# A mixture-of-experts kernel: first-layer products whose width follows the expert's token count

## The chip, the cores and the metric

The program runs on one core of a Trainium2 chip. The metric is device time in microseconds (us) for one execution; the smaller the better. TensorE (PE in the profile, with its weight loads shown apart as PEld) multiplies, ScalarE (ACT), VectorE (DVE) and GpSimd (POOL) work on tiles, and SyncE (SP) issues transfers. A `q` behind an engine's name in a row marks what its sequencer does itself: semaphore waits, register loads, branches.

## The reference

Three stages follow each other: an attention block (4 batches, 8 heads, 576 positions), a gated MLP, and a mixture of experts. The change lies in the last one:

```
logits = einsum('bsd,de->bse', x, w_gate)             # 8 experts
e = argmax(logits[b, s]), or the expert of the position before (sticky gate)
h = maximum(x[b, s] @ w1[e], 0.0)                     # 512 -> 1024, first layer
out[b, s] = p[e] * (h @ w2[e])                        # 1024 -> 512, second layer
```

There are 4 x 576 = 2304 tokens, and each goes to one of the 8 experts. How many an expert gets is known only when the program runs. Worked out with the reference on the inputs of its default seed, experts 0 to 7 get 227, 356, 289, 239, 277, 278, 294 and 344 tokens.

## The kernel before

Attention and the MLP fill the first two thirds of the span. In that time the routing of each batch (`route`) gives every token a place in its expert's list and adds the batch's counts to the tile `carry` (L1133; a row for each partition, summed over partitions by a product with ones). An expert has room for `CAP` = 3 blocks of 128 tokens, `CC` = 384 columns, in the static part; a loop at the end (`overflow`, L1190 and L1191) would handle what does not fit.

Per expert, `gather` fetches the 3 blocks of token rows by an indirect transfer on GpSimd's queue, `xT` transposes them on TensorE (L1287) into a rounded half and a rest (`xt[:, 0]`, `xt[:, 1]`), `L1` makes the first layer and `L2` the second. `L1` works in 8 groups of 128 hidden units; each group is one accumulation of 12 products (4 slices of the 512 inputs, 3 products each) over 384 columns, followed by Relu on ScalarE (L1300) and the rest on VectorE (L1301). `L2` works in 3 blocks of 128 tokens, each 24 products of 512 columns (L887 is the line of `mm3`, the helper that issues nearly all products), then a scaling on ScalarE and an indirect store. There are 7 rotating accumulator tiles (`ps`) and one for small results (`rt`, through `rs()`).

Weights come in pieces of 512 KB (`load_w`): a transfer into one of 2 raw tiles, a cast on ScalarE (L1256), the rest on VectorE (L1257), into one of 10 `wp` tiles; an expert has 8 pieces, 0 to 3 for the first layer, 4 to 7 for the second. Expert 0 is handled apart and early (2 blocks in `early_L1`, the third by `L1_rows`); experts 1 to 7 run in the loop of `experts`. A scheduler orders each engine's instructions by data and by order of emission; in the program text all 4 first-layer pieces of expert e + 1 follow `L1` of expert e, and its 4 second-layer pieces follow `L2`.

Of the kernel before, what the change touches and what calls it, by code (L numbers as in the profile page):

```python
# [8 lines left out]
F32 = mybir.dt.float32  # L9
F32R = mybir.dt.float32r  # L10
BF16 = mybir.dt.bfloat16
I32 = mybir.dt.int32
ACTF = mybir.ActivationFunctionType
ALU = mybir.AluOpType
# [10 lines left out]
def f32v(ap):  # L25
    return ap.bitcast(F32)
# [7 lines left out]
def kernel(  # L34
# [19 lines left out]
    PE, ACT, DVE, POOL, SP = nc.tensor, nc.scalar, nc.vector, nc.gpsimd, nc.sync  # L54
# [5 lines left out]
    E = w_gate.shape[1]  # L60
# [4 lines left out]
    KD = DM // 128  # L65
# [16 lines left out]
    def behind(x, name):  # L82

        tc.add_manual_dep(
            x.ins, name, mybir.DependencyInfo(mybir.DependencyClass.NoSync, mybir.DependencyReason.DATA), reason="after"
        )
# [8 lines left out]
    def ps(tag="ps", bufs=7):  # L95
        t = psum.tile([128, 512], F32, tag=tag, name=tag, bufs=bufs)
        return t

    def rs():
        return ps("rt", 1)  # L100
# [15 lines left out]
    def T(pool, shape, dt, tag, bufs=1):  # L116
        _n[0] += 1
        return pool.tile(shape, dt, tag=tag, name=f"{tag}_{_n[0]}", bufs=bufs)
# [19 lines left out]
    onesb = T(const, [128, 128], BF16, "onesb")  # L138
# [5 lines left out]
    carry = T(const, [128, E], BF16, "carry")  # L144
# [740 lines left out]
    def mm3(pt, pairs, first_, last_):  # L885
        n = len(pairs)
        ms = [PE.matmul(pt, lhsT=l, rhs=r, start=(first_ and x == 0), stop=(last_ and x == n - 1)) for x, (l, r) in enumerate(pairs)]  # L887
        return ms
# [353 lines left out]
    WP = {}  # L1242

    def load_w(e, j):

        r = T(wpool, [128, 1024], F32, "wraw", bufs=2)
        if j < KD:
            dma(r, w1[e, 128 * j:128 * j + 128, :])
        else:
            f0 = 256 * (j - KD)  # L1250
            x = dma(r.rearrange("p (a d) -> p a d", a=2), w2[e, f0:f0 + 256, :].rearrange("(a p) d -> p a d", p=128))
            if e == 0:
                behind(x, m_loads[LPN])
        near = (e * 2 * KD + j) % (WA + WB) < WA
        w = T(wpool if near else epool[0], [128, 2, 1024], F32R, "wp", bufs=WA if near else WB)
        c = ACT.copy(out=w[:, 0, :], in_=r)  # L1256
        a = DVE.tensor_tensor(out=w[:, 1, :], in0=r, in1=f32v(w[:, 0, :]), op=ALU.subtract)  # L1257
        if (0, KD) <= (e, j) < (1, KD):
            behind(a, dmarks[-1].ins.name)
        if (1, 0) < (e, j) < (1, 2 * KD):  # L1260
            behind(c, amarks[1 if j < KD else 3].ins.name)
        WP[e, j] = w

    CC = CAP * 128
# [10 lines left out]
    def gather(e):  # L1275
        for blk in range(CAP):
            c = e * NBLK + blk
            x = fetch(xgs[e % 2][:, blk, :], ids[:, c:c + 1])
        return x.ins.name

    def xT(xt, xg, n0, n):

        w = 128 * n
        for kt in range(KD):
            pt = ps()
            for blk in range(n):
                PE.transpose(pt[:, 128 * blk:128 * blk + 128], xg[:, n0 + blk, 128 * kt:128 * kt + 128], ident)  # L1287
            ACT.copy(out=xt[:, 0, kt, 0:w], in_=pt[:, 0:w])
            DVE.tensor_tensor(out=xt[:, 1, kt, 0:w], in0=pt[:, 0:w], in1=f32v(xt[:, 0, kt, 0:w]), op=ALU.subtract)

    def L1(e, xt, ht, w_, after={}):
        for f in range(NF):
            pt = ps()
            fs = slice(128 * f, 128 * f + 128)
            for kt in range(KD):
                w = WP[e, kt]
                ms = mm3(pt[:, 0:w_], [(w[:, 0, fs], xt[:, 0, kt, 0:w_]), (w[:, 0, fs], xt[:, 1, kt, 0:w_]), (w[:, 1, fs], xt[:, 0, kt, 0:w_])], kt == 0, kt == KD - 1)
                if kt == 0 and f in after:
                    behind(ms[0], after[f].ins.name)
            ACT.activation(out=ht[:, 0, f, 0:w_], in_=pt[:, 0:w_], func=ACTF.Relu)  # L1300
            DVE.scalar_tensor_tensor(out=ht[:, 1, f, 0:w_], in0=pt[:, 0:w_], scalar=0.0, in1=f32v(ht[:, 0, f, 0:w_]), op0=ALU.max, op1=ALU.subtract)  # L1301
            yield 12 * w_ * 0.42

    def L2(pool, e, ht, t, prob, idx):
        of = out.rearrange("b s d -> (b s) d")
        pt = ps()
        ts_ = slice(128 * t, 128 * t + 128)
        for f in range(NF):
            w = WP[e, KD + f // 2].rearrange("p z (a d) -> p z a d", a=2)[:, :, f % 2, :]
            mm3(pt, [(ht[:, 0, f, ts_], w[:, 0, :]), (ht[:, 0, f, ts_], w[:, 1, :]), (ht[:, 1, f, ts_], w[:, 0, :])], f == 0, f == NF - 1)  # L1310
        y = T(pool, [128, DM], F32, "y", bufs=3)
        ACT.activation(out=y, in_=pt, func=ACTF.Copy, scale=prob)  # L1312
        POOL.indirect_dma_start(  # L1313
            out=of[:, :], out_offset=bass.IndirectOffsetOnAxis(ap=idx, axis=0), in_=y, in_offset=None,
            bounds_check=NT - 1, oob_is_err=False,
        )
# [27 lines left out]
    def L1_rows(pool, e, xt, ht):  # L1344

        hs = []
        for z in range(2):
            fs = slice(512 * z, 512 * z + 512)
            pt = ps()
            for kt in range(KD):  # L1350
                w = WP[e, kt]
                mm3(pt, [(xt[:, 0, kt, 0:128], w[:, 0, fs]), (xt[:, 0, kt, 0:128], w[:, 1, fs]), (xt[:, 1, kt, 0:128], w[:, 0, fs])], kt == 0, kt == KD - 1)
            hs.append(T(pool, [128, 512], F32, "y", bufs=3))
            amarks.append(ACT.activation(out=hs[z], in_=pt, func=ACTF.Relu))
            yield 1
        for z in range(2):
            pt = ps()
            for f in range(4):
                PE.transpose(pt[:, 128 * f:128 * f + 128], hs[z][:, 128 * f:128 * f + 128], ident)
            pv = pt.rearrange("p (f t) -> p f t", f=4)  # L1360
            d = slice(4 * z, 4 * z + 4)
            amarks.append(ACT.copy(out=ht[:, 0, d, 0:128], in_=pv))
            DVE.tensor_tensor(out=ht[:, 1, d, 0:128], in0=pv, in1=f32v(ht[:, 0, d, 0:128]), op=ALU.subtract)  # L1363
            yield 1

    def next_w(e, js):
        for j in js:
            if e < E and (e, j) not in WP:
                load_w(e, j)

    def experts(pool):
        xts = {}

        def new_xT(e, n0=0):
            xts[e] = T(pool, [128, 2, KD, CC], F32R, "xT", bufs=2)
            xT(xts[e], xgs[e % 2], n0, CAP - n0)

        def new_hT():
            return T(pool, [128, 2, NF, CC], F32R, "hT", bufs=1)

        def early_L2(t):
            L2(pool, 0, early["ht"], t, early["xg"][:, t, DM:DM + 1], ids0[:, t:t + 1])

        next_w(0, range(2 * KD))
        early_L2(0)
        xts[0] = T(pool, [128, 2, KD, CC], F32R, "xT", bufs=2)
        xT(xts[0], early["xg2"].unsqueeze(1), 0, 1)
        ht0 = new_hT()
        rows = L1_rows(pool, 0, xts[0], ht0)
        next(rows), next(rows)  # L1390
        early_L2(1)
        next(rows), next(rows)
        for e in range(E):
            if 0 < e < E - 1:
                g = gather(e + 1)
            if e == 3:
                emit_olist(pool, g)
            xt = xts.pop(e)
            t0 = 0 if e else CAP - 1
            ht = new_hT() if e else ht0  # L1400
            if e:
                for _ in L1(e, xt, ht, CC):
                    pass
            for j in range(KD):
                WP.pop((e, j))
            if e + 1 < E:
                next_w(e + 1, range(KD))
                new_xT(e + 1)
            for t in range(t0, CAP):
                c = e * NBLK + t  # L1410
                xg = xgs[e % 2][:, t] if e else early["xg2"]
                L2(pool, e, ht, t - t0, xg[:, DM:DM + 1], ids[:, c:c + 1])
            for j in range(KD):
                WP.pop((e, KD + j))
            next_w(e + 1, range(KD, 2 * KD))

    def merge(a, b, ra, rb):

# [15 lines left out]
    def W_steps():  # L1434
        yield from emit_w_in(0)
        store(None, 0)
        yield from emit_w_in(1)
        store(None, 0)
        emit_consts2()
        emit_gl()  # L1440
# [37 lines left out]
    w = W_steps()  # L1478
# [7 lines left out]
    for b in range(B - 1):  # L1486
        m = M_steps(b) if b else M0_steps()
# [34 lines left out]
    x = fetch(early["xg2"], ids[:, CAP - 1:CAP])  # L1522
    for z in (1, 0):
        behind(POOL.memset(xgs[z], 0.0), x.ins.name)
    gather(1)
    experts(epool[0])
    ectx.close()
    wctx.close()
# [30 lines left out]
```

## Time and profile before

| what | us |
|---|---|
| median of 3 runs | 804.86 |
| lowest and highest run | 803.7 and 806.03 |
| the profiled execution's own time | 809.9 |
| its span, first to last instruction | 808.0 |
| TensorE busy in the span | 782.2 |
| VectorE, ScalarE, GpSimd busy | 519.7, 436.4, 333.7 |

The profile shows one execution. Times in its rows count from the start of the span. Ends of matmuls are modelled and neighbours overlap, so the pace of TensorE is read from start to start, not from the length of one matmul.

### The profile page before, as it was taken

To read this page: it belongs to the slowest core of one execution; us is meant where nothing else is said; L and a number is where in the kernel's file an instruction comes from. 1 tells how busy PE (TensorE), PEld (TensorE's weight loads), DVE (VectorE), ACT (ScalarE), POOL (GpSimd) and SP (SyncE) were. 2 spreads that over 40 slices of the span, in tenths; PEclk is the share of its full clock that TensorE was granted. 3 is DMA by queue.
4 is the path that set the end of the run, shared out by engine and by line. 5 is a ranking of instruction groups with operands and counts; after the bars stand their busy time and mean duration, and the time that the engine had idled before them with its cause. 6 is when DMAs were issued, how large, how long until landed. Compare 5 with 4: busy or idle time off the path is not lost. (4 is left out here: it accounts for less than half of the span.)

```text
span 808.0 us, 14644 instructions
## 1 busy us (share of the span) xinstructions
PE 782.2 (97%) x4818; PEld 672.3 (83%) x4818; DVE 519.7 (64%) x1474; ACT 436.4 (54%) x1040; POOL 333.7 (41%) x609
## 2 busy tenths in 40 slices
PE   8998998999999999999999999999999999999995
PEld 4676787799898899788898878788898989989894
DVE  4888477885776988696985876755534535344420
ACT  4777677875446876266962463145444444344410
POOL 5678646775535687245873020160122130411101
PEclk6999999999999999999999999999999999999998
DMA  6698599666688595686623950165445353634301
GB/s 155 166 244 246 151 251 267 163 188 158 148 263 206 111 250 116 166 252 165 160 99 103 332 183 8 63 220 189 163 159 165 121 191 107 210 133 142 132 2 37
DMA packets 118041, 133.06 MB, mean 165 GB/s; under 512 B 69603, under 2 KB 83043, under 8 KB 117963
## 3 DMA queue, kind: packets, MB, share of 16 engines
q1 hardware_dynamic: 114123, 122.61, 53.8%
q0 software_dynamic: 3840, 9.48, 3.2%
q8 instruction: 40, 0.66, 0.3%
q14 instruction: 38, 0.31, 0.1%
HBM read 90.99 MB, written 22.95 MB: 141 GB/s over the span
## 5 line engine op out<-in xcount | busy, mean ns | idle before, releaser
L1257 DVE TENSOR_TENSOR wp<-wraw,wp 128x1024 fp32r<-128x1024 f32 x64 | 77.7, 1224 | 98.1 <-ACT wp L1256 97.3
L887 PE MATMUL ps<-wp,hT 128*128 128x512 f32 x528 | 123.3, 393 | 1.1 <-DVE hT L1363 0.6
L887 PE MATMUL ps<-xT,wp 128*128 128x384 f32 x672 | 119.2, 336 | 0.0
L887 PEld LDWEIGHTS ps<-xT,wp 128*128 128x128 f32 x672 | 117.3, 188 | 0.7
L887 PEld LDWEIGHTS ps<-wp,hT 128*128 128x128 f32 x528 | 98.5, 188 | 22.8 <-DVE hT L1363 1.1
L1313 POOL DMA_INDIRECT out_dram<-y,ids x24 | 27.0, 1124 | 212.9 <-ACT y L1312 181.7
L1256 ACT CAST wp<-wraw 128x1024 fp32r<-128x1024 f32 x64 | 66.4, 1049 | 60.1 <-DMA wraw<-in_moe_w_dram 53.0
L447 ACT ACTIVATE E<-E,negm 128x128 f32<-128x128 f32 (+4 forms) x136 | 79.2, 583 | 34.3 <-DVE negm L440 22.3
L451 POOL TENSOR_SCALAR E<-E,lsum 128x128 f32<-128x128 f32 (+4 forms) x136 | 80.9, 598 | 35.4 <-DVE lsum L449 28.6
L572 PE MATMUL ps<-et,vv 128*128 128x320 f32 (+9 forms) x462 | 79.0, 308 | 2.3 <-DVE et L539 1.2
L440 DVE CUSTOM_DVE_ANT_0 E<-ps,zmask 128x128 f32<-128x128 f32 (+4 forms) x136 | 63.6, 471 | 26.6 <-PE ps L887 17.6
L572 PEld LDWEIGHTS ps<-et,vv 128*128 128x128 f32 (+1 forms) x462 | 62.5, 171 | 15.4 <-DVE et L539 1.7
L532 PE MATMUL ps<-ident,E 128*128 128x128 f32 (+1 forms) x452 | 67.5, 261 | 3.3 <-POOL E L451 1.6
L448 POOL TENSOR_SCALAR lsum<-lsum 128x1 f32<-128x1 f32 (+1 forms) x128 | 30.3, 237 | 95.8 <-ACT E L447 82.9
L887 PE MATMUL ps<-wsg,vg 128*128 128x288 f32 x448 | 67.5, 300 | 0.6 <-DVE g L896 0.3
L541 ACT CAST et<-ps 128x384 fp32r<-128x384 f32 (+3 forms) x120 | 50.5, 428 | 28.5 <-PE ps L532 27.3
L887 PEld LDWEIGHTS ps<-wsg,vg 128*128 128x128 f32 x448 | 61.0, 188 | 1.4 <-DVE g L896 0.6
L542 DVE TENSOR_TENSOR et<-ps,et 128x384 fp32r<-128x384 f32 (+3 forms) x120 | 56.8, 481 | 3.9 <-ACT et L541 3.6
L532 PEld LDWEIGHTS ps<-ident,E 128*128 128x128 f32 (+1 forms) x452 | 47.1, 140 | 13.8 <-POOL E L451 3.4
L1301 DVE SCALAR_TENSOR_TENSOR hT<-ps,hT 128x384 fp32r<-128x384 f32 x56 | 30.4, 553 | 42.5 <-ACT hT L1300 42.3
L887 PE MATMUL ps<-w,vg 128*128 128x512 f32 (+1 forms) x216 | 56.9, 403 | 0.0
L887 PE MATMUL ps<-xh,w 128*128 128x288 f32 x240 | 54.3, 303 | 1.0 <-DVE wsg L870 0.7
(315 smaller groups left out, 1580.6 us busy)
## 6 DMA issues: line engine op xcount, KB each, us to landing
wraw<-in_moe_w_dram SPq DMA_DIRECT2D x64, 512.0 KB
qk<-qk SPq DMA_DIRECT2D x24, 432.0 KB
w<-wv_d SPq DMA_DIRECT2D x16, 512.0 KB
w<-wo_d SPq DMA_DIRECT2D x16, 512.0 KB
qk<-qk SPq DMA_DIRECT2D x24, 288.0 KB
w<-wu_d SPq DMA_DIRECT2D x11, 512.0 KB
nq<-in_q_dram SPq DMA_DIRECT2D x30, 144.0 KB
nk<-in_k_dram SPq DMA_DIRECT2D x30, 144.0 KB
```

The source lines that it names most:

```text
L440: hred[g] = DVE.tensor_tensor_reduce(out=e[:, a:z], in0=pt[:, 0:z - a], in1=zmask[:, m0:m0 + z - a], scale=-1.0, scalar=BIG if hi == 0 els ...
L447: ACT.activation(out=x, in_=x, func=ACTF.Exp, scale=-1.0, bias=nm, accum_out=l[:, z:z + 1])
L448: POOL.tensor_scalar(out=l, in0=l, scalar1=1e-9, scalar2=0.0, op0=ALU.add, op1=ALU.add)
L451: POOL.tensor_scalar(out=x, in0=x, scalar1=l[:, z:z + 1], scalar2=1.0, op0=ALU.mult, op1=ALU.mult)
L532: PE.transpose(pt[:, j * M:(j + 1) * M], e[h, 128 * j:128 * (j + 1)], ident[h, h])
L541: ACT.copy(out=dst[0], in_=src)
L542: DVE.tensor_tensor(out=dst[1], in0=src, in1=f32v(dst[0]), op=ALU.subtract)
L572: PE.matmul(x, lhsT=l, rhs=rhs if g >= F4 else f32v(rhs), start=(j == 0 and n_ == 0), stop=(j == js[-1] and n_ == len(ms) - 1),)
L887: ms = [PE.matmul(pt, lhsT=l, rhs=r, start=(first_ and x == 0), stop=(last_ and x == n - 1)) for x, (l, r) in enumerate(pairs)]
L1256: c = ACT.copy(out=w[:, 0, :], in_=r)
L1257: a = DVE.tensor_tensor(out=w[:, 1, :], in0=r, in1=f32v(w[:, 0, :]), op=ALU.subtract)
L1301: DVE.scalar_tensor_tensor(out=ht[:, 1, f, 0:w_], in0=pt[:, 0:w_], scalar=0.0, in1=f32v(ht[:, 0, f, 0:w_]), op0=ALU.max, op1=ALU.subtract)
```

## The change

Before the loop over experts, a new `emit_wide` sums `carry` over partitions (one small product), turns the count of each expert into a class 0 to 3 on VectorE (up to 256, 288, 320 tokens, or more), and loads the classes of experts 1 to 7 into seven TensorE registers. `L1` of these experts then holds each group of 12 products in four versions, 256, 288, 320 and 384 columns wide, and TensorE picks one by two nested tests of its register. The first product of a group stays 384 columns wide in all versions, so that the whole accumulator is defined. Relu, the rest, `L2` and expert 0 keep their widths. The emission of weight pieces moves: pieces 6 and 7 of expert e now stand inside its own `L1` (after groups 0 and 2), pieces 0 and 1 of expert e + 1 too (after groups 4 and 6), pieces 2 and 3 stay behind `L1`, 4 and 5 behind `L2`.

```diff
+    LW = (0, 2, 4, 6)
+    WIDE = (256, 288, 320, CC)
+    wide = {}
+    def emit_wide(pool):
+        pt = rs()
+        PE.matmul(pt[:, 0:E], lhsT=onesb, rhs=carry, start=True, stop=True)
+        cls = T(pool, [128, 2, E], F32, "cls")
+        cli = T(pool, [128, E], I32, "cli")
+        DVE.tensor_copy(out=cls[:, 0], in_=pt[:, 0:E])
+        DVE.tensor_scalar(out=cls[:, 1], in0=cls[:, 0], scalar1=float(WIDE[0]), scalar2=None, op0=ALU.is_gt)
+        for x in WIDE[1:-1]:
+            DVE.scalar_tensor_tensor(out=cls[:, 1], in0=cls[:, 0], scalar=float(x), in1=cls[:, 1], op0=ALU.is_gt, op1=ALU.add)
+        DVE.tensor_copy(out=cli, in_=cls[:, 1])
+        for e in range(1, E):
+            wide[e] = PE.value_load(cli[0:1, e:e + 1])
...
-            for kt in range(KD):
-                w = WP[e, kt]
-                ms = mm3(pt[:, 0:w_], [(w[:, 0, fs], xt[:, 0, kt, 0:w_]), (w[:, 0, fs], xt[:, 1, kt, 0:w_]), (w[:, 1, fs], xt[:, 0, kt, 0:w_])], kt == 0, kt == KD - 1)
...
+            def products(c):
+                pairs = []
+                for kt in range(KD):
+                    w = WP[e, kt]
+                    pairs += [(w[:, 0, fs], 0, kt), (w[:, 0, fs], 1, kt), (w[:, 1, fs], 0, kt)]
+                for n, (l, z, kt) in enumerate(pairs):
+                    a = w_ if n == 0 else c
+                    m = PE.matmul(pt[:, 0:a], lhsT=l, rhs=xt[:, z, kt, 0:a], start=(n == 0), stop=(n == len(pairs) - 1))
...
+            if e in wide:
+                def choose(a, z):
+                    if z - a == 1:
+                        products(WIDE[a])
+                        return
+                    m = (a + z) // 2
+                    with tc.If(wide[e] < m) as x:
+                        choose(a, m)
+                    with x.Else():
+                        choose(m, z)
+                choose(0, len(WIDE))
+            else:
+                products(w_)
...
+        emit_wide(pool)
         for e in range(E):
...
-                for _ in L1(e, xt, ht, CC):
-                    pass
+                for f, _ in enumerate(L1(e, xt, ht, CC)):
+                    if f in LW:
+                        n = 2 * KD * e + 2 * KD - 2 + LW.index(f)
+                        next_w(n // (2 * KD), (n % (2 * KD),))
...
-            next_w(e + 1, range(KD, 2 * KD))
+            next_w(e + 1, range(KD, 2 * KD - 2))
```

## Rows read from the trace of the kernel before

**Rows 1.** The page: its span, busy times, granted clock, instruction queue (packets, MB, share).

```profile
span 808.0 us, 14644 instructions
PE 782.2 (97%) x4818; PEld 672.3 (83%) x4818; DVE 519.7 (64%) x1474; ACT 436.4 (54%) x1040; POOL 333.7 (41%) x609
PEclk6999999999999999999999999999999999999998
q8 instruction: 40, 0.66, 0.3%
```

**Rows 2.** Busy time by stage: expert 2's first layer, second layer, expert 7's first.

```profile
core 0: us, PE busy (x) PEld busy (x) DVE busy (x) ACT busy (x) POOL busy (x), PEclk, DMA share, GB/s
...
591.00:608.00 17.00, 17.00 (x102) 16.96 (x101) 7.06 (x10) 7.97 (x13) 2.06 (x2) 1.00 0.40 135
608.00:626.00 18.00, 18.00 (x86) 15.03 (x84) 8.61 (x11) 7.95 (x12) 4.36 (x4) 1.00 0.57 180
...
765.00:782.00 17.00, 17.00 (x99) 16.92 (x99) 3.90 (x7) 4.46 (x9) 0.98 (x1) 1.00 0.02 6
```

**Rows 3.** TensorE in order of time, experts 2 and 7: start, length, line, shape, count.

```profile
590.63 16.83 PE L887 MATMUL ps<-xT,wp 128*128 128x384 f32 x96
607.30 1.47 PE L1287 MATMUL ps<-ident,xg 128*128 128x128 f32 x12
608.53 16.74 PE L887 MATMUL ps<-wp,hT 128*128 128x512 f32 x72
...
764.82 16.83 PE L887 MATMUL ps<-xT,wp 128*128 128x384 f32 x96
781.48 16.65 PE L887 MATMUL ps<-wp,hT 128*128 128x512 f32 x72
```

**Rows 4.** TensorE in order of time: dense stretches of narrower and of small products.

```profile
481.66 14.29 PE L887 MATMUL ps<-wsg,vg 128*128 128x288 f32 x106 [0.33 <-DVE g L896]
495.79 0.70 PE L887 MATMUL ps<-vg,wgl 128*18 128x288 f32 x4
...
515.35 0.20 PE L1098 MATMUL rt<-carry,onesb 128*128 128x40 bf16 x1
515.73 4.57 PE L887 MATMUL ps<-xTA,wp 128*128 128x256 f32 x36
522.06 7.45 PE L887 MATMUL ps<-xTA,wp 128*128 128x256 f32 x60
529.35 2.04 PE L887 MATMUL ps<-wp,hTA 128*128 128x512 f32 x8
```

**Rows 5.** TensorE in order of time, where the new loads would come.

```profile
546.60 1.03 PE L1359 MATMUL ps<-ident,y 128*128 128x128 f32 x8
547.47 1.47 PE L1287 MATMUL ps<-ident,xg 128*128 128x128 f32 x12
549.40 0.73 PE L887 MATMUL ps<-wp,hT 128*128 128x512 f32 x2 [0.46 <-ACT hT L1362]
550.78 3.02 PE L887 MATMUL ps<-wp,hT 128*128 128x512 f32 x12 [0.65 <-DVE hT L1363]
```

**Rows 6.** TensorE's sequencer: branches, register load, one semaphore wait (min/median/max ns).

```profile
L1191 PEldq COMPARE_BRANCH  x3: 97/179/408, 794.6 to 803.3; - x3
L1190 PEldq TENSOR_LOAD <-olist x1: 485/485/485, 793.9 to 793.9; - x1
L1287 PEldq EVENT_SEMAPHORE  x1: 51/51/51, 604.2 to 604.2; - x1
```

**Rows 7.** All engines in order of time at the end of the products.

```profile
793.62 4.51 PE L887 MATMUL ps<-wp,hT 128*128 128x512 f32 x19
798.22 0.69 ACT L1312 ACTIVATE y<-ps,xg 128x512 f32<-128x512 f32 x1 [4.80 <-PEq L1191]
```

**Rows 8.** Small operations on the counts: a product with ones, VectorE on `carry`.

```profile
L1323 PE MATMUL rt<-carry,onesb x1: 177/177/177, 467.5 to 467.5; 128*128 128x1 bf16 x1
L1133 DVE TENSOR_TENSOR carry<-carry,oh x20: 144/153/164, 223.3 to 517.2; 128x8 bf16<-128x8 bf16 x16, 64x8 bf16<-64x8 bf16 x4
```

**Rows 9.** Groups of the page: weight casts and the work behind each first-layer group.

```profile
L1257 DVE TENSOR_TENSOR wp<-wraw,wp 128x1024 fp32r<-128x1024 f32 x64 | 77.7, 1224 | 98.1 <-ACT wp L1256 97.3
L1256 ACT CAST wp<-wraw 128x1024 fp32r<-128x1024 f32 x64 | 66.4, 1049 | 60.1 <-DMA wraw<-in_moe_w_dram 53.0
L1301 DVE SCALAR_TENSOR_TENSOR hT<-ps,hT 128x384 fp32r<-128x384 f32 x56 | 30.4, 553 | 42.5 <-ACT hT L1300 42.3
```

**Rows 10.** Waits of 545 to 808 us: Relu, and the cast for its transfer.

```profile
ACT hT L1300 <- PE ps L887: 49.7, 34, 2.6
ACT wp L1256 <- DMA wraw<-in_moe_w_dram: 37.6, 27, 3.3
```

**Rows 11.** The chain that ended last, in order of time: start, length, what.

```profile
794.75 4.20 issue
```

More of the change, by code (lines that the diff above doesn't have):

```diff
@@ L1294, in L1 @@
             fs = slice(128 * f, 128 * f + 128)
-            for kt in range(KD):
-                w = WP[e, kt]
-                ms = mm3(pt[:, 0:w_], [(w[:, 0, fs], xt[:, 0, kt, 0:w_]), (w[:, 0, fs], xt[:, 1, kt, 0:w_]), (w[:, 1, fs], xt[:, 0, kt, 0:w_])], kt == 0, kt == KD - 1)
-                if kt == 0 and f in after:
-                    behind(ms[0], after[f].ins.name)
+            def products(c):
[6 more added lines that the diff above has]
+                    m = PE.matmul(pt[:, 0:a], lhsT=l, rhs=xt[:, z, kt, 0:a], start=(n == 0), stop=(n == len(pairs) - 1))
+                    if n == 0 and f in after:
+                        behind(m, after[f].ins.name)
+            if e in wide:
[11 more added lines that the diff above has]
+                products(w_)
             ACT.activation(out=ht[:, 0, f, 0:w_], in_=pt[:, 0:w_], func=ACTF.Relu)
```

## The prediction

> **What bounds the kernel now.** I read the page first [rows 1]: TensorE is busy 97% of the span at full granted clock, no other engine above 64%. A share over the whole span proves nothing for one stage, so next I read the stages of the experts [rows 2]: in a first-layer stretch of 17 us TensorE is busy for all 17, VectorE for 7.06 and ScalarE for 7.97, the transfers have 40% of their time, and the clock is 1.00. Then TensorE in order of time [rows 3]: expert 2's 96 first-layer products start at 590.63, its 12 transposes at 607.30, its second layer at 608.53, with no idle time written beside any of them. Expert 7 looks the same. The waits [rows 10] turn it around: Relu waits for TensorE, 49.7 us in all. So in experts 1 to 7 TensorE sets the end, one group after the other, and time taken from its products is time taken from the kernel, as long as its sequencer, its weights and its code keep up.
>
> **What narrower products give back.** Paces are from start to start. At 384 columns: (607.30 - 590.63) / 96 = 173.6 ns [rows 3]. At 288, the MLP's 106 products in a row: (495.79 - 481.66) / 106 = 133.3 ns. At 256, expert 0's early first layer: (529.35 - 522.06) / 60 = 121.5 ns [rows 4]. So the pace follows the columns (0.42 ns for each between 288 and 384) and the weight load, 128 columns in every case, does not hold it up. No row has 320 columns in this stage; on the line between 288 and 384 it is 146.7 ns.
>
> The counts of the reference's default inputs give the classes: experts 1 and 7 (356, 344 tokens) 384; experts 2 and 6 (289, 294) 320; expert 3 (239) 256; experts 4 and 5 (277, 278) 288. In a group 11 of 12 products get narrower, 8 groups an expert: 88 products. Experts 2 and 6: 88 x 26.9 ns = 2.37 us each. Expert 3: 88 x 52.1 = 4.58. Experts 4 and 5: 88 x 40.3 = 3.55 each. Together 16.4 us. Expert 2 is one token above a border; one class lower it would give 1.2 us more.
>
> **Finding the classes.** The product with ones (177 ns in its like) and five small VectorE operations (153 ns in their like, 0.77 us) [rows 8] lie beside other work; VectorE may be in a weight rest when they come, 1.22 us [rows 9]. The seven register loads are TensorE's own. One took 485 ns [rows 6], so 3.4 us, during which the sequencer issues nothing; behind it stand the transposes and second layer of the last block of expert 0, and behind those everything else. How far does the sequencer run ahead? The one register load of before ran at 793.9 while products went on to 798.13 [rows 6, 7]: 17 products, 4.2 us, were already queued. A wait ahead of expert 3's transposes ran at 604.2, the transposes at 607.30: 3.1 us, 18 products. So a full queue hides most of 3.4 us. But where the loads come it holds short transposes, and TensorE already idles there for 0.46 and 0.65 us for another reason [rows 5], which swallows as much again. Lower end 0. Upper end, when the loads meet an empty queue and an unfinished class: 3.4 + 0.18 + 0.77 + one rest of 1.22 = 5.6 us. I take 2.0, nearer the lower end, because the row's own load was hidden.
>
> **Choosing, 56 times.** A path through a group has two tests and at most two jumps. TensorE's three branches took 97, 179 and 408 ns [rows 6]. Four of them: 0.39 us at the least, 0.91 at the mean of 228, 1.63 at the most. Issuing 12 products with their weight loads: the fastest stretch has 8 small products between 515.35 and 515.73 [rows 4], 47.5 ns each, so at most 0.57 us for 12. The sequencer needs 0.96 to 2.20 us for a group, 1.48 in the middle. TensorE's array needs 2.08 us at 384 columns, 1.79 at 320, 1.64 at 288 and 1.51 at 256 (one product at 173.6 and 11 at the pace above). In the middle all is hidden. At the upper end the sequencer falls behind by 0.69 us a group at 256, 0.56 at 288, 0.41 at 320; over 8 groups that is 5.5, 4.5 and 3.3 us, against a lead of 4.2 us that every second layer rebuilds: exposed 1.3 + 2 x 0.3 = 1.9 us in all. I take 0, with 1.9 as the upper end where branches only hold the sequencer. That a branch lets queued products go on is seen once: the first of the three ran at 794.6, inside the gapless products up to 798.13 [rows 6, 7].
>
> [...]
>
> **Moves that I cost at nothing.** The weight pieces change place in ScalarE's, VectorE's and SP's order. An expert's period was 34.5 us (590.63 to 625.1, the end of the second layer that starts at 608.53 [rows 3]) and falls to about 30 to 32; 8 casts of 1.05 us and 8 rests of 1.22 fit with the rest [rows 2, 9]. Pieces 6 and 7, now emitted after groups 0 and 2, are needed only after the other six groups, the transposes and 12 second-layer products (12 x 0.23 us), so over 8 us later, while the longest wait of a cast for its transfer was 3.3 us [rows 10]. A cast that waits holds up the Relu queued behind it on ScalarE, but 7 accumulators give TensorE some six groups, 9 us, before it feels that. If the cover went, a late piece would cost 3.3 + 1.05 + 1.22 = 5.6 us of TensorE for an expert. What comes after the experts is unchanged: products, store and the closing loop run as before, only earlier.
>
> **The sum.** 809.9 - 16.4 + 2.0 = 795.5 us on the profiled execution. That execution was 5.0 us above the median of the runs; on the median it is 804.86 - 14.4 = 790.5 us.
>
> **Rivals.**
>
> *Code arrives late (slower).* Three of four versions are stepped over: 96 instructions stand for 24 that run. The instruction queue that can only be TensorE's by its size brought 40 packets [rows 1] for 2 x 4818 instructions, one for 241. A first-layer stretch grows to some 8 x 101 instructions, 3.4 packets in 12 to 17 us, where there was one in 20. If each then stopped the sequencer for what the longest unexplained stop of the chain shows, 4.2 us [rows 11], the stretch would need 8 x 1.48 + 3.4 x 4.2 = 26.1 us against TensorE's 12.1 to 16.7 plus its lead of 4.2: 5.2 us lost at 384, 7.6 at 320, 8.8 at 288, 9.8 at 256, together 53, and the time about 843 us. It decides from about 2.6 us a packet, where the loss reaches 14.4. For it: nothing jumps in the code of before, so nothing shows that fetching keeps up. Against it: the packets are only 0.3% of the transfer time [rows 1], and a version not taken is at most 72 instructions, less than a packet.
> [...]
>
> *Each choice empties TensorE (slower).* If entering or leaving a version waits for running products, or the first product waits late for its accumulator, every group pays a restart. TensorE's idle times for a late hand-over were 0.46 and 0.65 us [rows 5]; 56 of them are 25.8 to 36.4 us, 816 to 827 us. It decides from 14.4 / 56 = 0.26 us. The branch at 794.6 speaks against it, but it had no join behind products.
>
> *Partly exposed (still faster).* The loads cost 5.6 instead of 2.0 us, branches 1.9, or a tenth of a microsecond shows in each group (5.6): 793 to 802 us.
>
> *No gain.* If the run's counts lie above 320 for nearly every expert, no product gets narrower, and the loads and branches leave 805 to 808 us.
>
> **Chances.** Forecast, 786 to 793 us: 0.64. Partly exposed, 793 to 802: 0.12. No gain, or costs that just eat it: 0.05. Emptied: 0.07. Late code: 0.12. About 0.3%, 2.4 us, is what a measurement of this kernel tells from no change. Faster is 0.76 (the first two), same 0.05, slower 0.19. The range runs from 786 (loads at no cost, the lowest run's 1.2 us, a class less for expert 2) to 808, where the two slower rivals begin; it leaves out most of these, a little under 2 in 10. The forecast's own range is 786 to 793.
>
> **What would show it.** Right: products of 256, 288 and 320 columns at 121 to 147 ns from start to start; first layers of about 12.1, 13.1, 14.3 and 16.7 us, back to back; no idle time between groups beyond a tenth of a microsecond; one stop of at most 5.6 us around the seven loads; second layers unchanged; some 17 to 24 more packets on the instruction queue. Wrong: idle time ahead of the first product of each group (emptied), or of 1 us and more in every second or third group with a packet just before it (late code), a first layer that waits for a weight piece, a granted clock below 1.00 in the experts, or more columns than the counts ask for.

## The result, and the profile after

The changed kernel takes 794.79 us in the median of 4 runs (793.36 to 797.54), the kernel before 805.44 in the median of 4. The ratio is 0.9865, 95% interval 0.982 to 0.9911: faster by 10.65 us, 7.2 to 14.5. The forecast was 790.5 with a range of 786 to 808; the forecast's own part of it ended at 793, so that the time lies just inside the part of the rival "partly exposed" (793 to 802).

The page of the changed kernel, beside [rows 1]:

```profile
span 795.7 us, 14829 instructions
PE 766.3 (96%) x4819; PEld 657.3 (83%) x4819; DVE 517.2 (65%) x1479; ACT 433.2 (54%) x1040; POOL 333.9 (42%) x609
PEclk9989989999999999999999999999999999999998
q8 instruction: 57, 0.93, 0.5%
```

TensorE's busy time fell by 15.9 us, the span by 12.3, and 17 more packets came on the instruction queue (forecast: 17 to 24; both from one profiled execution of each kernel). The products of the experts by shape, idle time at the right:

```profile
L1321 PE MATMUL ps<-xT,wp 128*128 128x384 f32 x232 | 47.8, 338 | 3.3 <-ACT y L1351 3.3
L1321 PE MATMUL ps<-xT,wp 128*128 128x320 f32 x176 | 28.4, 309 | 0.0
L1321 PE MATMUL ps<-xT,wp 128*128 128x288 f32 x176 | 25.9, 295 | 0.0
L1321 PE MATMUL ps<-xT,wp 128*128 128x256 f32 x88 | 11.8, 283 | 0.0
```

The classes are those of the counts: two experts at 320, two at 288, one at 256, and at 384 the first product of all 56 groups with 2 x 88 others. One thing is new: 3.3 us of idle time ahead of products of 384 columns, waiting for the second layer's scaled output `y` on ScalarE. TensorE in order of time, where [rows 3] had 96 first-layer products, 12 transposes and 72 second-layer products, each in one piece:

```profile
589.03 9.10 PE L1321 MATMUL ps<-xT,wp 128*128 128x384 f32 x60
597.97 2.00 PE L887 MATMUL ps<-wp,hT 128*128 128x512 f32 x8
599.81 1.95 PE L1321 MATMUL ps<-xT,wp 128*128 128x384 f32 x12
601.59 0.40 PE L887 MATMUL ps<-wp,hT 128*128 128x512 f32 x1
602.82 3.84 PE L1321 MATMUL ps<-xT,wp 128*128 128x384 f32 x24 [0.83 <-ACT y L1351]
...
769.37 16.65 PE L887 MATMUL ps<-wp,hT 128*128 128x512 f32 x72
```

(The merged rows name the first shape alone.) The last 9 second-layer products of expert 1 now stand inside the first layer of expert 2, the very last one ahead of its seventh group. ScalarE in the same stretch:

```profile
589.23 1.05 ACT L1256 CAST wp<-wraw 128x1024 fp32r<-128x1024 f32 x1 [1.17 <-DMA wraw<-in_moe_w_dram]
602.08 0.69 ACT L1351 ACTIVATE y<-ps,xg 128x512 f32<-128x512 f32 x1 [11.79 <-PE ps L887]
602.66 0.86 ACT L1339 ACTIVATE hT<-ps 128x384 fp32r<-128x384 f32 x2
```

The scaling of expert 1's last block stands in ScalarE's queue ahead of expert 2's Relus, and it waits 11.79 us for that last product. Meanwhile six groups fill six accumulators and the block holds the seventh; TensorE goes on at 602.82, when the scaling has ended at 602.77. From the start of the last product to the next it takes 1.23 us instead of the usual 0.23. The trace has four such places, behind experts 1 to 4. The sequencer's own work in the changed kernel:

```profile
L1331 PEldq COMPARE_BRANCH  x152: 65/180/1902, 553.6 to 764.5; - x152
L1307 PEldq TENSOR_LOAD <-cli x7: 304/311/482, 553.0 to 748.6; - x7
```

The register loads do not stand in one block: the scheduler put each ahead of its expert's first layer.

For the comparisons below, runs are also compared by the stretch of the experts: from the start of expert 1's first layer (the row of 95 or 96 products) to the start of expert 7's second layer. The part ahead of it varies by several us between executions of one and the same program; expert 1 began at 556.43 in one execution of the changed kernel and at 549.50 in another, and the stretch was 212.9 us in both. Before, it ran from 556.10 to 781.48, 225.4 us. (Where the row has 95 products, one of 0.17 us lies ahead of the stretch: before, e2_fixed and e4_move.) The first rows of the stretch, before and with the change:

```profile
556.10 16.83 PE L887 MATMUL ps<-xT,wp 128*128 128x384 f32 x95
...
556.43 16.97 PE L1321 MATMUL ps<-xT,wp 128*128 128x384 f32 x96
```

The medians in the table below are over all runs; its ratios compare means of undisturbed runs (three slow ones, of e4_move, e9_six and the kernel before, are left out) with the kernel before run beside that kernel, whose medians were 805.4 to 807.5 us, and so they are not quotients of two medians of the table.

### The profile page after: what moved, and what is told of

Read it like the earlier page. It is cut to its first block, busy times and chain, and to the rows that moved or that the text cites. A ratio compares the mean times of both kernels' runs of the same rounds, so it can differ in the third digit from the quotient of the medians.

```text
span 795.7 us, 14829 instructions
## 1 busy us (share of the span) xinstructions
PE 766.3 (96%) x4819; PEld 657.3 (83%) x4819; DVE 517.2 (65%) x1479; ACT 433.2 (54%) x1040; POOL 333.9 (42%) x609
## 5 line engine op out<-in xcount | busy, mean ns | idle before, releaser
L887 PE MATMUL ps<-wp,hT 128*128 128x512 f32 x528 | 125.4, 394 | 0.9 <-DVE hT L1402 0.6
L887 PEld LDWEIGHTS ps<-wp,hT 128*128 128x128 f32 x528 | 98.1, 188 | 21.8 <-DVE hT L1402 1.1
L1321 PE MATMUL ps<-xT,wp 128*128 128x384 f32 (+3 forms) x672 | 102.8, 312 | 3.3 <-ACT y L1351 3.3
L1321 PEld LDWEIGHTS ps<-xT,wp 128*128 128x128 f32 x672 | 101.2, 188 | 5.5 <-ACT y L1351 4.7
L572 PE MATMUL ps<-et,vv 128*128 128x320 f32 (+9 forms) x462 | 82.8, 319 | 2.2 <-DVE et L539 1.2
L572 PEld LDWEIGHTS ps<-et,vv 128*128 128x128 f32 (+1 forms) x462 | 65.0, 177 | 16.7 <-issue 3.0
```

Source lines behind the costliest of these rows:

```text
L572: PE.matmul(x, lhsT=l, rhs=rhs if g >= F4 else f32v(rhs), start=(j == 0 and n_ == 0), stop=(j == js[-1] and n_ == len(ms) - 1),)
L1321: m = PE.matmul(pt[:, 0:a], lhsT=l, rhs=xt[:, z, kt, 0:a], start=(n == 0), stop=(n == len(pairs) - 1))
```

## The experiments

| kernel | median us | ratio to before, 95% | stretch us |
|---|---|---|---|
| before | 805.44 | | 225.4 |
| the change | 794.79 | 0.9865 (0.982 to 0.9911) | 212.9 |
| e11_again, the change once more | 792.81 | 0.9831 (0.9802 to 0.9861) | 212.9 |
| e1_order | 788.3 | 0.9773 (0.9729 to 0.9816) | 208.4 |
| e2_fixed | 788.94 | 0.9795 (0.9739 to 0.985) | 208.9 |
| e3_all384 | 805.31 | 0.9975 (0.994 to 1.001) | 225.5 |
| e4_move | 804.5 | 0.9959 (0.9926 to 0.9991) | 225.4 |
| e5_eight | 829.09 | 1.0305 (1.0268 to 1.0342) | 249.9 |
| e6_twice | 831.66 | 1.0306 (1.0268 to 1.0345) | 251.3 |
| e7_four | 815.24 | 1.0106 (1.0076 to 1.0137) | 232.0 |
| e8_free384 | 816.99 | 1.0124 (1.0092 to 1.0156) | 232.2 |
| e9_six | 804.55 | 0.997 (0.9945 to 0.9996) | 223.1 |
| e10_nomove | 787.95 | 0.9772 (0.9743 to 0.98) | 208.5 |

The fences show each edit against e1_order, apart from those of e1_order and e2_fixed (against the changed kernel) and e4_move (against the kernel before).

**e1_order.** One order more: a first layer begins behind the second layer of the expert before.

```diff
+    last2 = []
...
-                def choose(a, z):
+                def choose(a, z, top=False):
...
                     with tc.If(wide[e] < m) as x:
+                        if top and f == 0 and last2:
+                            tc.add_manual_dep(x.cond_inst, last2[-1].ins.name, mybir.DependencyInfo(mybir.DependencyClass.NoSync, mybir.DependencyReason.DATA), reason="after")
...
-                choose(0, len(WIDE))
+                choose(0, len(WIDE), True)
...
-            mm3(pt, [(ht[:, 0, f, ts_], w[:, 0, :]), (ht[:, 0, f, ts_], w[:, 1, :]), (ht[:, 1, f, ts_], w[:, 0, :])], f == 0, f == NF - 1)
+            last2[:] = mm3(pt, [(ht[:, 0, f, ts_], w[:, 0, :]), (ht[:, 0, f, ts_], w[:, 1, :]), (ht[:, 1, f, ts_], w[:, 0, :])], f == 0, f == NF - 1)
```

> The changed kernel with one more order: the first group of an expert's first layer may not be placed ahead of the last second-layer product of the expert before. Theory A (the changed kernel loses its 4 stops of 1.0 us only because the last second-layer products were placed late, so that ScalarE's queue stood still behind them): the 4 stops go, 794.8 - 4.1 = 790.7 us, about 14.7 below the kernel before, and no idle time over 0.4 us ahead of any first-layer group. Rival B (the stop belongs to choosing a version, and appears wherever the sequencer has lost its lead): 794 to 795 us, stops of the same length at other groups.

788.3 us. Theory A holds, B falls. TensorE in order of time: the start of expert 1, experts 2 and 3, the end of the stretch:

```profile
551.01 16.97 PE L1322 MATMUL ps<-xT,wp 128*128 128x384 f32 x96
...
585.69 14.46 PE L1322 MATMUL ps<-xT,wp 128*128 128x384 f32 x96
599.99 1.47 PE L1287 MATMUL ps<-ident,xg 128*128 128x128 f32 x12
601.22 16.74 PE L887 MATMUL ps<-wp,hT 128*128 128x512 f32 x72
617.79 12.06 PE L1322 MATMUL ps<-xT,wp 128*128 128x384 f32 x96
629.69 1.04 PE L1287 MATMUL ps<-ident,xg 128*128 128x128 f32 x8
630.48 3.23 PE L887 MATMUL ps<-wp,hT 128*128 128x512 f32 x13
...
759.45 16.65 PE L887 MATMUL ps<-wp,hT 128*128 128x512 f32 x72
```

The layers of expert 2 are in one piece again, no second-layer product stands inside a first layer, and no stop is written. The first layers take 16.8, 14.3, 11.9, 13.1, 13.1, 14.3 and 16.7 us from their start to the transposes or second layer behind them, which is what the prediction listed. The stretch is 4.5 us shorter than with the change alone, four stops of 1.0 us and slightly slower products right behind each (behind the first, 24 products in 606.50 - 602.82 = 3.68 us, where the medians of 174 and 147 ns give 3.58). This kernel beats both.

**e2_fixed.** The same widths without counting, loading or testing.

```diff
-            if e in wide:
...
-                choose(0, len(WIDE))
+            if e:
+                products(FIXED[e])
```

> The widths 384, 320, 256, 288, 288, 320, 384 are written into the program for experts 1 to 7: no count is read, no class loaded, no test or jump; so this kernel is right for these inputs only. Theory A: 805.4 - 16.4 = 789.0 us, and the kernel with tests and the order (e1_order) lies within 1.7 us of it. Rival B: the tests cost something of their own; then e1_order lies 4 us or more above this one.

788.94 us, a stretch of 208.9: 16.5 below before, forecast 16.4. The bounds of the stretch, and the one stop in it:

```profile
551.82 16.83 PE L1307 MATMUL ps<-xT,wp 128*128 128x384 f32 x95
...
626.17 0.78 PE L1171 MATMUL rt<-ident,lf 1*120 1x1 f32 x6 [0.61 <-DVE lf L1165]
...
760.72 16.65 PE L887 MATMUL ps<-wp,hT 128*128 128x512 f32 x72
```

With the order pinned, reading the counts and choosing 56 times costs nothing that can be measured (e1_order even has 0.5 us less in the stretch; here expert 3's first layer stops once for 0.61 us for a small VectorE result, which in e1_order falls into the second layer).

**e3_all384.** Choosing without narrowing.

```diff
-                        products(WIDE[a])
+                        products(CC)
```

> The changed kernel with the order of e1_order and all four versions 384 columns wide: it reads the counts, loads the classes, tests and jumps as the changed kernel, and saves nothing. Theory A: 805.4 to 806.5 us, no change that can be measured, with TensorE dense in the first layers. Rival B: 809 us and more, the price of choosing laid bare.

805.31 us and a stretch of 225.5 against 225.4, from 552.78 to 778.32:

```profile
552.78 16.97 PE L1322 MATMUL ps<-xT,wp 128*128 128x384 f32 x96
...
778.32 16.65 PE L887 MATMUL ps<-wp,hT 128*128 128x512 f32 x72
```

The price of 56 choices among four versions is 0.1 us or nothing: the one product more in this stretch takes 0.17 us. That it is nothing with narrower products too, which leave the sequencer less time, is what e1_order beside e2_fixed shows (stretches of 208.4 and 208.9 us).

**e4_move.** The kernel before with the new places of the weight pieces; **e10_nomove**, e1_order with the old ones.

```diff
-                for _ in L1(e, xt, ht, CC):
-                    pass
+                for f, _ in enumerate(L1(e, xt, ht, CC)):
+                    if f in (0, 2, 4, 6):
+                        n = 2 * KD * e + 2 * KD - 2 + f // 2
+                        next_w(n // (2 * KD), (n % (2 * KD),))
...
-            next_w(e + 1, range(KD, 2 * KD))
+            next_w(e + 1, range(KD, 2 * KD - 2))
```

> The kernel before with only the new places of the weight pieces. Theory A: 804.5 to 806.5 us, as before, since no product waits for a weight in either. Rival C (part of the gain comes from earlier weights): 803 us or less.

> e1_order with the weight pieces emitted where the kernel before has them. Theory A (no product waits for a weight in either place): 788 to 790 us, as e1_order. Rival H (between groups that the scheduler treats as units, pieces 6 and 7 come late for the second layer): 792 us and more, with second-layer products that wait for a weight.

804.5 and 787.95 us, stretches of 225.4 and 208.5: both as their partners. The first one's ratio lies a little under 1, but its stretch does not differ, so nothing of it belongs to the weights. So the move is worth nothing in either direction.

**e8_free384.** e3_all384 without the order.

> e3_all384 without the order of e1_order: four versions, all 384 columns wide, the scheduler free. It places the last second-layer product of experts 1 to 6 inside the next first layer. Theory A (the stop belongs to that place alone): six stops of 1.0 us, 6 us more than e3_all384, about 811 us. Rival B (the stop needs narrow products): as e3_all384, 805 us.

816.99 us, more than expected; the stretch, 232.2 us, is 6.7 above e3_all384, as expected. Six stops again, one of them:

```profile
603.04 0.40 PE L887 MATMUL ps<-wp,hT 128*128 128x512 f32 x1
604.26 4.44 PE L1321 MATMUL ps<-xT,wp 128*128 128x384 f32 x24 [0.83 <-ACT y L1351]
```

So the stop belongs to the place of that product, not to narrow products, and not to the test alone (e3_all384 has the tests and no stop). Another 3.3 us stand ahead of the stretch in the profiled execution; the rest of the difference is open.

**e5_eight and e6_twice.** Eight versions and three tests, with the widths 240 to 384 and with those of e1_order.

```diff
-    WIDE = (256, 288, 320, CC)
+    WIDE = (240, 256, 272, 288, 304, 352, 368, CC)
+    ASKED = (256, 256, 288, 288, 320, CC, CC, CC)
...
-                        products(WIDE[a])
+                        products(ASKED[a])
```

(The line with `ASKED =` and the last two stand in e6_twice only.)

> e1_order with eight versions instead of four (240, 256, 272, 288, 304, 352, 368, 384 columns; three tests a group). Experts 1, 2, 3 and 6 get 16 columns narrower, expert 7 32: 6 x 88 x 16 x 0.42 ns = 3.5 us more. Theory A (TensorE's queued products hide tests and code): 788.3 - 3.5 = 784.8 us. Rival D (twice the code makes the sequencer late, some 17 packets of instructions become about 40, and the 0.4 to 1.9 us that some branches took in the changed kernel add up): no gain over e1_order, 788 to 796 us, with idle time ahead of groups.

> The eight versions and three tests of e5_eight, but with only the widths of e1_order (256, 256, 288, 288, 320, 384, 384, 384): the price of the second half of the code by itself. Theory A: 788.3 us, as e1_order within a microsecond. Rival D: 791 to 800 us.

829.09 and 831.66 us: theory A falls, and rival D is right in kind and far too small, 41 and 43 us above e1_order. The instruction queue on e5_eight's page (packets, MB, share):

```profile
q8 instruction: 80, 1.31, 0.7%
```

Its branches (min/median/max ns):

```profile
L1332 PEldq COMPARE_BRANCH  x224: 65/176/4048, 548.0 to 798.8; - x112
```

And TensorE's waits from 545 to 800 us (total, times, longest):

```profile
PE ps L1322 <- issue: 13.1, 11, 2.3
PE ps L1322 <- ACT hT L1342: 10.3, 8, 1.5
```

The median branch is as short as in the change, but 31 of them took 1.7 to 4.0 us, 77.9 us together. In the trace every one of these ends 2.3 to 3.0 us behind the start of a packet of the instruction queue. That fits a sequencer that stands at a jump until the code behind it has come; no row names what it waits for. "issue" is a stop that waits for nothing the profile shows; where ScalarE is named, its Relu had only ended last and was not what was missing: it had ended 0.6 to 1.0 us before the product, and a branch 0.06 us before it. In all, 28 stops of TensorE add up to 31.0 of the 41.5 us by which the stretch is longer than e1_order's.

**e7_four.** Four choices a group, three products each: more tests, hardly more code.

```diff
-            def products(c):
+            def products(c, part):
...
+                    if kt not in part:
+                        continue
...
-                choose(0, len(WIDE), True)
+                for kt in range(KD):
+                    choose(0, len(WIDE), (kt,), kt == 0)
```

> e1_order with four choices in each group instead of one, each for 3 of the 12 products. In the changed kernel the recorded branches add up to 33.2 us, 0.59 us for a choice. Four make 2.4 us, with 0.57 us to issue 12 products 2.9 us a group, more than the 1.51 to 2.08 us that TensorE needs, so the queue runs empty: 8 groups fall behind by 6.8 to 11.3 us, less the 4.2 us lead. Theory A (choosing is hidden only while the sequencer is faster than the array): 34 us more than e1_order with those numbers, 808 to 823 us if issuing is faster than its bound, and idle time at every choice. Rival E (branches cost TensorE nothing at any number): 788 to 790 us.

815.24 us, 27 above e1_order, inside the range. Its branches:

```profile
L1334 PEldq COMPARE_BRANCH  x608: 65/176/579, 551.7 to 785.3; - x152
```

Not one is long, with 61 packets. The first layers of experts 3 and 5, and what stands behind each:

```profile
625.84 14.73 PE L1324 MATMUL ps<-xT,wp 128*128 128x384 f32 x96
640.41 1.04 PE L1287 MATMUL ps<-ident,xg 128*128 128x128 f32 x8
...
696.62 7.56 PE L1324 MATMUL ps<-xT,wp 128*128 128x384 f32 x48
704.53 10.93 PE L1324 MATMUL ps<-xT,wp 128*128 128x288 f32 x48 [0.36 <-issue]
715.30 1.47 PE L1287 MATMUL ps<-ident,xg 128*128 128x128 f32 x12
```

The branches take 98.1 us together in the trace, but not the same in every expert: 1.86 us a group in expert 5 and 1.30 in expert 3. With the prediction's bound of 0.57 us for issuing that is 2.43 and 1.87 us, and their groups took (715.30 - 696.62) / 8 = 2.34 and (640.41 - 625.84) / 8 = 1.82, where the products alone need 1.64 and 1.51. Little of it is written as idle time; it shows in the pace from start to start. So there are two prices in these runs: each test cost the sequencer its time (a branch 0.18 us in the median), which showed here, where a group's tests and issues took longer than its products, and not in e3_all384; and the long branches came with the code (up to 4.05 us in e5_eight, 224 branches and 80 packets), not with the number of tests (0.58 us at most here, 608 branches).

**e9_six.** Six versions.

```diff
-    WIDE = (256, 288, 320, CC)
+    WIDE = (256, 288, 304, 352, 368, CC)
```

> e1_order with six versions (256, 288, 304, 352, 368, 384 columns). Experts 1, 2 and 6 get 16 columns narrower, expert 7 32: 5 x 88 x 16 x 0.42 ns = 3.0 us of products less than e1_order. Theory F (TensorE's code comes in packets no closer than 3.0 us; a group may not step over more code than arrives in its own time, plus one lead of 4.2 us for each expert): some 11 more packets than e1_order's 57; 5 packets a first layer, so 15 to 17 us for each, against 12 to 16.1 us of products plus the lead: the gain shrinks to nothing in the narrow experts and the wide ones keep it, 786 to 793 us, with stops of at most 1.5 us in experts 3 to 5. Rival G (the third test, not the code, was what cost 41 us in e5_eight): 808 us and more. Rival A (no price below eight versions): 785.3 us, no stops.

804.55 us: between A and G, as F would have it, but F's range is missed by 11 us or more. TensorE in order of time, expert 3, and the packets of that first layer:

```profile
621.62 4.62 PE L1322 MATMUL ps<-xT,wp 128*128 128x384 f32 x36
628.07 9.19 PE L1322 MATMUL ps<-xT,wp 128*128 128x384 f32 x60 [1.83 <-issue]
638.48 1.06 PE L1287 MATMUL ps<-ident,xg 128*128 128x128 f32 x8 [1.22 <-DVE wp L1257]
...
q8 instruction: 4, 0.07, 1.7%
```

The first layers took 14.3 to 18.5 us, 16.4 in the mean, where F had 15 to 17; expert 3's took 16.9 instead of 11.9. F's lengths were near, with 4 to 5 packets in each; its mistake was to count the lead of 4.2 us against them, of which the lengths show nothing. Its stops of at most 1.5 us were exceeded too (1.83 above).

**e11_again.** The change once more.

> The changed kernel once more, on the chip of these runs, for a comparison with e1_order's neighbours: 793 to 797 us, four stops of 1.0 us ahead of a first-layer group that wait for the scaled output on ScalarE.

792.81 us, a little under what was expected, with the same four stops and the same stretch.

## Why the prediction was right, step by step

**Narrower products: right.** From start to start the medians are 147, 132 and 120 ns at 320, 288 and 256 columns (146.7, 133.3 and 121.5 in the prediction), and e2_fixed shows the sum, 16.5 us for 16.4.

**Finding the classes: over-sized.** 2.0 us were set aside for seven loads in a block. They stand one by one ahead of their experts, 0.30 to 0.48 us each, 3.4 to 4.1 us before the first layer begins, and cost nothing that e3_all384 could show.

**Choosing: right.** 0.1 us or nothing in e3_all384, nothing in e1_order beside e2_fixed. The branches of the changed kernel add up to 32.7 us, 0.58 us a group where the prediction had 0.91 in the middle.

**"Moves that I cost at nothing": the step that failed.** The weight moves do cost nothing (e4_move, e10_nomove). But the step, and the sentence that products run as before, left out that the place of a group with versions among the second-layer products could change. It did for four experts, and because ScalarE took its queue in order, a single product that came late held up every Relu behind it: five groups of expert 2 were done by 597.97, and its first Relu ran at 602.66. The prediction had named this chain, for a cast that comes late, with a cover of six groups, 9 us; the wait here was 11.79 us. One of its signs of being right, no idle time between groups beyond a tenth of a microsecond, failed at these four places. The loss is 4.5 us (e1_order against the change), and with e8_free384 it is shown to be the order. e2_fixed has neither tests nor the pinned order and no such place, so the new order came with the tests. Why the scheduler chose it was not tried; in the rows the second-layer products stand only between whole groups of 12.

**The sum.** 16.4 - 2.0 = 14.4 was forecast. In the stretch 12.5 us came out: 16.5 or a little more from narrower products, 0 for loads and tests, 4.5 lost to the order. The two errors partly cancelled. The medians' 10.65 us have an interval that holds both. That the time lies inside 786 to 808 is in part luck: the room from 793 to 802 was made for loads, branches and a tenth of a microsecond in each group, none of which was paid, and the loss that was paid is in no term.

**The rivals.** "Each choice empties TensorE" is refuted for choosing (e2_fixed, e3_all384); its price, an accumulator that comes late, was paid at 4 groups instead of 56. "Code arrives late" did not decide at four versions, but at eight came stops that fit it. The rival put a stop at 4.2 us and needed 2.6 us for every packet to decide; the 31 stops of the sequencer in e5_eight took 2.5 us in the mean. With four versions a first layer of e1_order takes in 3 to 4 packets in 11.9 to 16.8 us, and no stop of TensorE is written; five branches of the change took 0.85 to 1.9 us, each ending 2.3 to 2.4 us behind the start of a packet, and the queued products hid them (TensorE's four stops are the ones above). With eight, six packets came in one first layer:

```profile
q8 instruction: 6, 0.10, 1.8%
```

(Instruction queue of e5_eight from 625.42 to 647.49, expert 3's first layer: 6 packets in 22.1 us.) The prediction held against this rival that a version not taken is less than a packet. In e5_eight the seven not taken are 168 instructions, still less than the 241 that the prediction worked out for a packet, and 31 branches took 1.7 to 4.0 us all the same. "Partly exposed" holds the measured time and not its cause, as said under the sum. "No gain" did not come: the classes are those of the counts.

## What to carry to other kernels

Versions chosen by a register can pay in full, as here in e1_order (17.0 us off the stretch): the tests of the changed kernel cost its sequencer 0.58 us a group, and queued products hid one choice a group (0.1 us or nothing in e3_all384), but not four (27 us in e7_four). Count the code stepped over, not only the tests: here four versions fitted, six ate the gain and eight cost 41 us more than four. After adding a choice, compare the order on the engine with the one before, and pin what has moved; here one late product in each of four experts, with ScalarE's queue standing behind it, took 4.5 of 17.0 us.

## What the runs showed of the hardware beyond that

The packets of the instruction queue were nowhere closer than 3.0 us from the experts on, in any of the kernels (3.13 in the change), and mostly 3.0 to 3.6 us apart in the first layers of e6_twice and e9_six, though a packet itself took from 0.9 us; what sets that distance is open. And a stretch with stops of TensorE had one with a lower clock behind it. A table of stretches of e5_eight: length, busy times, granted clock.

```profile
633.00:640.00 7.00, 4.49 (x34) 4.13 (x35) 1.85 (x5) 2.50 (x5) 0.27 (x2) 0.98 0.04 11
640.50:645.90 5.40, 4.93 (x23) 4.67 (x22) 2.36 (x3) 0.85 (x2) 0.00 (x0) 0.50 0.55 190
```

TensorE was busy 4.49 us of 7.00 in the first stretch; in the second the granted clock was 0.50, and the 240-column products came every 213 ns there. The second-layer products behind them were still slow, at a granted clock of 0.56 from 649.00 to 654.00:

```profile
649.08 5.21 PE L887 MATMUL ps<-wp,hT 128*128 128x512 f32 x13
```

The same 13 products took 3.23 us in e1_order (the row from 630.48 above). That the idle time brought the lower clock is my reading; no run tried it.
